# One core, two linear-attention and FFN layer pairs: a new list-scheduling search, a third late q chunk, and the token sum of pk moved from TensorE to Pool

## The chip, the core and the metric

The kernel runs on one core of one Trainium2 chip. The metric is the device time of one execution in microseconds (us); lower is better. In this document PE is TensorE, ACT is ScalarE, DVE is VectorE and Pool is GpSimd.

## The reference

Four residual layers on x of 2048 tokens by 512 features, bf16: attention, FFN, attention, FFN, with the same weights both times (shortened here).

```python
def _A_ref(x, wqkv, wo):                      # H = 32 heads of 16
    q, k, v = ...                             # from x @ wqkv
    phi = lambda t: jnp.where(t > 0, t + 1, jnp.exp(t)) + 1e-6
    pq, pk = phi(q), phi(k)
    kv = jnp.einsum("bhsd,bhse->bhde", pk, v)
    z = jnp.einsum("bhsd->bhd", pk)           # the token sum
    num = jnp.einsum("bhqd,bhde->bhqe", pq, kv)
    den = jnp.einsum("bhqd,bhd->bhq", pq, z)[..., None] + 1e-6
    o = num / den
    return o.transpose(...).reshape(B, S, D) @ wo
# _B_ref: relu(x @ w1) @ w2, Dff = 1376
x = x + _A_ref(_layernorm(x), wqkv, wo)
x = x + _B_ref(_layernorm(x), w1, w2)
# ... and both once more
```

## The kernel before

All operations are collected in a graph with a cost in ns each, and a list scheduler written in Python decides, when the kernel is built, the order on each engine and the PSUM bank of each tile. It starts from the source order and alternates six backward and forward passes.

The tokens are 16 tiles of 128, in four chunks of four. An attention layer has a **key phase** (per tile: the k projection, its phi, and G += xn^T pk; early q chunks in between), a **barrier** (the token sum z, the evacuation of G, kv, Wp = kv @ wo, and the first denominators, none of which can start before the last key tile), and an output phase that overlaps the FFN. q chunks that are projected only in the barrier ("late") are there to give PE something to do. The first layer's key phase also holds the layer norm of the raw input.

phi is two ACT reads of the PSUM bank, then a clamp and a maximum on DVE:

```python
if path == 3:
    g.add(ACT, lambda e: e.activation(dst_ap, psv[:, b, :], ACTF.Identity, bias=1.0 + 1e-6, scale=1.0),
          [("ps", b)], [dst_key], C_ACT_PSUM, name=name + "_lin")
    g.add(ACT, lambda e: e.activation(escr[:, s, :], psv[:, b, :], ACTF.Exp),
          [("ps", b)], [("escr", s)], C_ACT_EXP, name=name + "_exp")
    g.add(DVE, lambda e: e.tensor_scalar(emscr[:, s, :], escr[:, s, :], 1.0, 1e-6, ALU.min, ALU.add),
          [("escr", s)], [("emscr", s)], C_DVE_BF4X, name=name + "_em")
    g.add(DVE, lambda e: e.tensor_tensor(dst_ap, dst_ap, emscr[:, s, :], ALU.max),
          [dst_key, ("emscr", s)], [dst_key], 340.0, name=name + "_phi")
    return
```

The token sum, 64 matmuls of one column per layer, and the barrier:

```python
def a_z_acc(lo, hi, zb):
    def mk():
        mms = []
        for i in range(lo, hi):
            u = pk_unit(i)
            for j in range(4):
                mms.append((psv[:, zb, j:j + 1], big[:, u * 512 + 128 * j:u * 512 + 128 * j + 128], ones[:, 0:1],
                            i == 0 and j == 0, i == NT - 1, True))
        return mms
    mm_group(mk, [("big", pk_unit(i)) for i in range(lo, hi)] + [("ones",)], [("ps", zb)], (hi - lo) * 4 * C_MMTINY, "z%d" % lo)
# [...]
def bar():
    if first_layer:
        den_consts()
    late = list(range(max(0, NCH - Q_LATE), NCH))
    for i in range(NT - LAG, NT):
        a_g_acc(i, GB)
    zb = alloc_bank()
    for k in range(NCH):
        a_z_acc(4 * k, 4 * k + 4, zb)
    a_z_final(zb)
    a_g_evac(GB)
    for t in late[:LATE_A]:
        a_q_proj(t, late=True)
    a_kv()
    for t in range(DEN_PRE):
        a_den(t, GB)
    for t in late[LATE_A:]:
        a_q_proj(t, late=True)
    a_wp()
```

Of the kernel before, what the change touches and what calls it, by code (L numbers as in the profile page):

```python
# [23 lines left out]
C_DVE_PSUM = 600.0  # L24
C_DVE_STT = 615.0
C_DVE_BF4X = 205.0
C_DVE_SMALL = 72.0
C_DVE_BNST = 595.0
C_DVE_NORM_BF = 325.0
C_POOL_POW = 1000.0  # L30
# [6 lines left out]
C_POOL_CP = 700.0  # L37
C_SP_ISSUE = 470.0
TAIL = {PE: 70.0, ACT: 230.0, DVE: 80.0, POOL: 300.0, SP: 0.0}
SYNC_LAT = 40.0  # L40
SLACK = {PE: 0.0, ACT: 0.0, DVE: 0.0, POOL: 0.0, SP: 0.0}


class _Op:
    __slots__ = ("eng", "emit", "reads", "writes", "dur", "lat", "sdeps", "odeps", "idx",
                 "seq", "dma", "name", "t_start", "t_done", "t_ready", "issued", "prio", "alts")

    def __init__(self, eng, emit, reads, writes, dur, lat, dma, name):
        self.eng = eng
        self.emit = emit  # L50
        self.reads = reads
        self.writes = writes
        self.dur = dur
        self.lat = lat
        self.dma = dma
        self.name = name
        self.sdeps = []
        self.odeps = []
        self.alts = None
        self.seq = None  # L60
        self.t_start = None
        self.t_done = None
        self.issued = False
# [100 lines left out]
def _forward(ops, succ, tile_ops, nbanks, fixed_sp):  # L164
# [36 lines left out]
    while remaining:  # L201
        best = None
        fr = sorted(x for x in bank_free if x is not None)
        for e in ENGINES:
            if not ready[e]:
                continue
            fa = free_at[e]
            cands = []
            for o in ready[e]:
                if e == SP and sp_next < len(fixed_sp) and o is not fixed_sp[sp_next]:  # L210
                    continue
                t = o.t_ready
                need = alloc_of.get(o.idx)
                if need:
                    if len(fr) < len(need):
                        continue
                    t = max(t, fr[len(need) - 1] + SYNC_LAT)
                st = max(t, fa)
                if o.alts:
                    mine = [d for (x, _, d) in o.alts if x == e][0]  # L220
                    worse = False
                    for (ae, _, adur) in o.alts:
                        if ae != e and max(t, free_at[ae]) + adur < st + mine - 1e-9:
                            worse = True
                    if worse:
                        continue
                cands.append((st, o))
            if not cands:
                continue
            st0 = min(c[0] for c in cands)  # L230
            lim = st0 + SLACK[e]
            st, o = min((c for c in cands if c[0] <= lim), key=lambda c: (-c[1].prio, c[1].idx))
            if best is None or st0 < best[0] - 1e-9 or (abs(st0 - best[0]) <= 1e-9 and o.idx < best[2].idx):
                best = (st0, st, o, e)
# [28 lines left out]
        if o.dma:  # L263
            dma_free = max(st + 1500.0, dma_free) + o.lat
            o.t_done = dma_free + 500.0
        else:
            o.t_done = st + o.dur + TAIL[e]
# [14 lines left out]

def _list_schedule(ops, tile_ops, vbank, fixed_sp, iters=6, nbanks=8):
    succ = _succs(ops)
    rank = {o.idx: float(o.idx) for o in ops}
    best = None
    for _ in range(iters):
        _backward(ops, succ, rank)
        res = _forward(ops, succ, tile_ops, nbanks, fixed_sp)
        if best is None or res[0] < best[0]:  # L290
            best = res
        for o in ops:
            rank[o.idx] = o.t_start
    total, order, vb, bank_after, snap = best
# [13 lines left out]

def build_kernel(nc, A_x, A_wqkv, A_wo, B_w1, B_w2, out, n_layers_pairs=2, Q_LATE=2, O_PE_CHUNKS=3, PHI_PATH=3,
                 KV_LAG=2, INTERLEAVE=True, WARM=16, SPLIT_CHUNKS=1, TAIL_SPLIT=True,  # L310
                 PHI_K=3, PHI_QE=3, PHI_QL=3, LAST_HALVES=True, ZH_FIRST=True, P2_TIGHT=False,
                 FIRST_PE_CHUNKS=1, TGK=2, TGF=2, WO_LAG=1, DEN_PRE=1, LATE_A=1, ITERS=6):
    S = A_x.shape[1]
# [13 lines left out]
    with es:  # L327
# [46 lines left out]
        rneg = sb("rneg", [128, 1], F32)  # L374
        Zc = sb("Zc", [128, 4, 32], BF16)
        GT = sb("GT", [128, 4, 512], BF16)
        KVT = sb("KVT", [128, 4, 128], BF16)
# [27 lines left out]

        def dma(emit, reads, writes, xfer_ns, name):
            sem = es.enter_context(nc.semaphore("dsem%d" % len(dma_sems)))
            dma_sems.append(sem)

            def _emit(eng, emit=emit, sem=sem):  # L410
                return emit(eng).then_inc(sem, 16)
            op = g.add(SP, _emit, reads, writes, dur=C_SP_ISSUE, lat=xfer_ns, dma=True, name=name)
            op.seq = sem
            return op

        def pk_unit(i):
            return (i % 4) * NCH + (i // 4)
# [21 lines left out]
        ld_x(0, 1)  # L439
        dma(lambda e: e.dma_start(wqkv[:, :, D:2 * D], wq_v[:, :, D:2 * D]), [], [("wk",)], 1600.0, "ld_wk")  # L440
        for t in range(1, NCH):
# [4 lines left out]
        dma(lambda e: e.dma_start(wo[:], A_wo.rearrange("(c p) n -> p c n", p=128)), [], [("wo",)], 1600.0, "ld_wo")  # L446
        early_loads = list(g.ops)
        nfull = NFC - 1 if FLAST < 128 else NFC
# [3 lines left out]
        if FLAST < 128:  # L452
            dma(lambda e: e.dma_start(w2[0:FLAST, NFC - 1, :], B_w2[nfull * 128:DFF, :]), [], [("w2b",)], 600.0, "ld_w2b")
        late_loads = g.ops[len(early_loads):]
        W2KEYS = [("w2a",), ("w2b",)] if FLAST < 128 else [("w2a",)]
# [65 lines left out]
        def tr_dma(lo, hi):  # L521
            dma(lambda e: e.dma_start_transpose(Tb[:, lo:hi, :, :].rearrange("p i c t -> p (i c) t"),
                                                xn[:, lo:hi, :].rearrange("p i d -> p (i d)")),
                [("xn", i) for i in range(lo, hi)], [("T", i) for i in range(lo, hi)], 740.0 * (hi - lo), "tr%d" % lo)

# [96 lines left out]
        def a_k_proj(i):  # L622
            b = alloc_bank()
            mm_group(lambda: [(psv[:, b, :], Tb[:, i, c, :], wqkv[:, c, D:2 * D], c == 0, c == 3, False) for c in range(4)],
                     [("T", i), ("wk",)], [("ps", b)], 4 * C_MM512, "kproj%d" % i)
            phi_evac(b, pk_tile(i), ("big", pk_unit(i)), "k%d" % i, path=PHI_K)

        def a_g_acc(i, GB):
# [4 lines left out]

        def a_z_acc(lo, hi, zb):
            def mk():
                mms = []
                for i in range(lo, hi):
                    u = pk_unit(i)
                    for j in range(4):
                        mms.append((psv[:, zb, j:j + 1], big[:, u * 512 + 128 * j:u * 512 + 128 * j + 128], ones[:, 0:1],  # L640
                                    i == 0 and j == 0, i == NT - 1, True))
                return mms
            mm_group(mk, [("big", pk_unit(i)) for i in range(lo, hi)] + [("ones",)], [("ps", zb)], (hi - lo) * 4 * C_MMTINY, "z%d" % lo)

# [27 lines left out]

        def a_wp():
            for j in range(4):
                b = alloc_bank()
                mm_group(lambda b=b, j=j: [(psv[:, b, :], KVT[:, j, :], wo[:, j, :], True, True, False)],
# [121 lines left out]
        def ln_tile_first(i):  # L798
            ln_stats_first(i)
            c = slice(i, i + 1)  # L800
            g.add(DVE, lambda e: e.tensor_scalar(veps[:, c], mv[:, i, 1:2], 0.0, EPS, ALU.max, ALU.add),
                  [("var", i)], [("veps1", i)], C_DVE_SMALL, name="veps%d" % i)
# [37 lines left out]
        def layer_steps(layer):  # L840
# [3 lines left out]
            if layer % 2 == 0:  # L844
# [13 lines left out]
                def bar():  # L858
# [5 lines left out]
                    zb = alloc_bank()  # L864
                    for k in range(NCH):
                        a_z_acc(4 * k, 4 * k + 4, zb)
                    a_z_final(zb)
# [6 lines left out]
                    for t in late[LATE_A:]:  # L874
                        a_q_proj(t, late=True)
                    a_wp()

                def p2(t):
                    if t < NCH and t >= DEN_PRE:
                        a_den(t, GB)  # L880
                    if t >= WO_LAG:
                        for i in range(4 * (t - WO_LAG), 4 * (t - WO_LAG) + 4):
                            a_wo(i, first_layer)
                        tr_chunk(t - WO_LAG, TGF)
                        ln_ffn(t - WO_LAG)
# [39 lines left out]

        order, total = _list_schedule(g.ops, g.tile_ops, vbank, early_loads + first_tr + late_loads, ITERS)
        for e in (PE, ACT, DVE, POOL):
            for k, o in enumerate(order[e]):
                o.seq = k + 1
# [27 lines left out]

        def emit_engine(e, handle):
            for o in order[e]:
                for d in waits[o.idx]:  # L960
                    if d.dma:
# [10 lines left out]
        with nc.Block() as block:  # L972
# [4 lines left out]
            @block.scalar  # L977
            def _(s):
                s.preload_act_table_set("natural_log_exp_and_others")
                emit_engine(ACT, s)  # L980
# [54 lines left out]
```

## Time and profile before

The median is 295.24 us (295.19 to 295.36), the span in the profile 293.0 us. The lines below are from the profile's page: busy time and share of the span of each engine, and in 40 slices of the span DVE's busy share and the TensorE clock granted, in tenths (9 is 90% or more). PE is busy nearly always, at full clock.

```profile
PE 282.9 (97%) x1470; PEld 129.3 (44%) x1491; DVE 164.0 (56%) x485; ACT 171.8 (59%) x349; POOL 20.7 (7%) x32
...
DVE  5998637996349551480326474599832955130233
...
PEclk9999999999999999999999999999999999999999
```

The next lines are from the PE timeline of before: start us, length us, engine, line, operation and operands, count, and in brackets the idle time before it with what ended it. The token sum occupies PE from 43.98 to the next group at 45.58, 1.60 us. The first barrier follows; at 48.94 and 62.29 PE had been waiting, the second time for 1.43 us.

```profile
43.98 1.74 PE L573 MATMUL ps<-ones,big 128*128 128x1 bf16 x64
45.58 1.05 PE L573 MATMUL ps<-GT,wqkv 128*128 128x128 bf16 x16
...
48.94 0.39 PE L573 MATMUL ps<-wo,KVT 128*128 128x512 bf16 x1 [0.36 <-DVE Wp L652]
...
60.47 0.40 PE L573 MATMUL ps<-big,Zc 128*32 128x512 bf16 x4
62.29 1.89 PE L573 MATMUL ps<-Wp,big 128*128 128x512 bf16 x8 [1.43 <-DVE emscr L557]
```

The view of waits, for PE alone (total us, number of times, longest): it sums both barriers. It counts only time in which no matmul was being executed; by start-to-start distances beyond the regular 0.216 us of a 512-column matmul, PE lost 2.6 us in each barrier.

```profile
PE ps L573 <- DVE emscr L557: 2.9, 2, 1.4
...
PE ps L573 <- DVE Wp L652: 0.7, 2, 0.4
```

The windows view gives the busy us of each engine in stretches of the span (start:end, length, then engine by engine with the number of instructions). 8:44 is the first key phase, 44:66 and 184:206 the barriers.

```profile
core 0: us, PE busy (x) PEld busy (x) DVE busy (x) ACT busy (x) POOL busy (x), PEclk, DMA share, GB/s
8.00:44.00 36.00, 35.57 (x170) 16.03 (x172) 27.71 (x97) 27.82 (x54) 4.71 (x4) 1.00 0.68 187
44.00:66.00 22.00, 20.00 (x170) 9.38 (x171) 20.04 (x53) 19.17 (x42) 0.00 (x0) 1.00 0.25 26
...
184.00:206.00 22.00, 20.00 (x170) 9.43 (x170) 19.70 (x53) 18.84 (x41) 0.00 (x0) 1.00 0.16 25
```

In the groups of instructions (busy us, mean ns of one, then idle time before them), phi's maximum and clamp:

```profile
L559 DVE TENSOR_TENSOR big<-big,emscr 128x512 bf16<-128x512 bf16 x64 | 26.0, 422 | 3.9 <-ACT big L553 3.5
...
L557 DVE TENSOR_SCALAR emscr<-escr 128x512 bf16<-128x512 bf16 x64 | 17.8, 290 | 21.7 <-ACT escr L555 21.2
```

### The profile page before, as it was taken

What the parts mean: (1) busy time and instruction counts of PE and PEld (TensorE: products, weight loads), DVE (VectorE), ACT (ScalarE), POOL (GpSimd) and SP (SyncE); (2) the same over time, 40 slices, a digit from 0 to 9 for tenths busy, and PEclk for the clock granted to TensorE, in tenths of its full rate; (3) what the DMA queues carried; (4) which work ended last, traced back from release to release, by engine and by line L of the source; (5) the groups of instructions that cost most, each with busy time, mean ns of one, the idle gap of its engine ahead of it and who ended that gap; (6) DMA issues with size and microseconds to landing.
All of it is one profiled execution on the core that took longest, in us unless ns stands there. A gap on an engine that the chain in (4) does not pass through costs nothing.

```text
span 293.0 us, 4025 instructions
## 1 busy us (share of the span) xinstructions
PE 282.9 (97%) x1470; PEld 129.3 (44%) x1491; DVE 164.0 (56%) x485; ACT 171.8 (59%) x349; POOL 20.7 (7%) x32
## 2 busy tenths in 40 slices
PE   7999999989999999999999999998999999999996
PEld 2444445434444444444444444533444444444443
DVE  5998637996349551480326474599832955130233
ACT  1888757997664583597623486599766407317000
POOL 4213000002001110010001100000100011000000
PEclk9999999999999999999999999999999999999999
DMA  6945930073003070030000340004610424001022
GB/s 224 346 78 104 303 122 2 0 75 61 10 2 72 0 143 2 1 72 0 3 0 0 72 74 0 2 0 73 39 36 0 34 71 112 0 11 63 0 72 74
DMA packets 40163, 17.23 MB, mean 59 GB/s; under 512 B 31984, under 2 KB 39632, under 8 KB 40144
## 3 DMA queue, kind: packets, MB, share of 16 engines
q1 hardware_dynamic: 40144, 16.98, 26.7%
q8 instruction: 12, 0.20, 0.3%
q14 instruction: 7, 0.06, 0.1%
HBM read 7.01 MB, written 2.10 MB: 31 GB/s over the span
## 4 chain that ended last, share of the span: by engine, by line
PE 83%; DVE 11%; DMA 3%; issue 1%; SPq 0%
PE ps L573 83%; DVE big L720 3%; DMA xin<-in_A_x_dram 2%; DVE xres L586 2%; DMA Tb<-xn 1%; DVE big L559 1%; DVE Wp L652 1%; DVE bst L483 1%; DVE emscr L557 1%; DVE xn L593 1%; DVE rsp L714 1%; DVE rhi L713 0%; DVE xn L515 0%; DVE nmf L589 0%; DVE xin L760 0%
## 5 line engine op out<-in xcount | busy, mean ns | idle before, releaser
L573 PE MATMUL ps<-Tb,w 128*128 128x512 bf16 (+1 forms) x352 | 78.0, 379 | 0.0
L573 PE MATMUL ps<-w,big 128*128 128x512 bf16 (+3 forms) x355 | 76.4, 372 | 0.4
L741 ACT ACTIVATE big<-ps 128x512 bf16<-128x512 f32 (+1 forms) x81 | 48.2, 596 | 29.4 <-PE ps L573 28.9
L580 ACT ACTIVATE sqscr<-xres 128x512 bf16<-128x512 f32 x48 | 30.3, 635 | 42.7 <-DVE xres L617 27.9
L573 PEld LDWEIGHTS ps<-w,big 128*128 128x128 bf16 (+1 forms) x363 | 35.4, 98 | 40.8
L573 PEld LDWEIGHTS ps<-Tb,w 128*128 128x128 bf16 (+1 forms) x352 | 34.9, 100 | 40.9 <-issue 0.9
L555 ACT ACTIVATE escr<-ps 128x512 bf16<-128x512 f32 x64 | 38.4, 613 | 9.7 <-PE ps L573 9.7
L553 ACT ACTIVATE big<-ps 128x512 bf16<-128x512 f32 x64 | 38.3, 613 | 3.0 <-PE ps L573 3.0
L613 DVE SCALAR_TENSOR_TENSOR xin<-ps,rstdf,xres 128x512 bf16<-128x512 f32 x15 | 11.3, 750 | 38.5 <-PE ps L573 38.5
L573 PE MATMUL ps<-wqkv,Tb 128*128 128x512 bf16 x125 | 31.4, 379 | 0.3
L573 PE MATMUL ps<-Wp,big 128*128 128x512 bf16 x124 | 28.7, 379 | 3.0 <-DVE emscr L557 2.9
L573 PE MATMUL ps<-big,xn 128*128 128x512 bf16 x124 | 31.3, 379 | 0.2
L573 PE MATMUL ps<-Tb,wqkv 128*128 128x512 bf16 x128 | 30.5, 380 | 0.1
L557 DVE TENSOR_SCALAR emscr<-escr 128x512 bf16<-128x512 bf16 x64 | 17.8, 290 | 21.7 <-ACT escr L555 21.2
L559 DVE TENSOR_TENSOR big<-big,emscr 128x512 bf16<-128x512 bf16 x64 | 26.0, 422 | 3.9 <-ACT big L553 3.5
L617 DVE SCALAR_TENSOR_TENSOR xres<-ps,rstdf,xres 128x512 f32<-128x512 f32 x16 | 12.0, 751 | 24.8 <-PE ps L573 24.8
L720 DVE TENSOR_TENSOR big<-big,ps 128x512 bf16<-128x512 bf16 x32 | 20.1, 681 | 7.9 <-PE ps L573 7.9
L573 PEld LDWEIGHTS ps<-Wp,big 128*128 128x128 bf16 x128 | 12.2, 98 | 17.6 <-DVE big L720 3.0
L573 PEld LDWEIGHTS ps<-big,xn 128*128 128x128 bf16 x128 | 12.5, 98 | 15.1 <-DVE big L559 0.2
L573 PEld LDWEIGHTS ps<-wqkv,Tb 128*128 128x128 bf16 x128 | 12.2, 98 | 15.2 <-DMA Tb<-xn 0.6
L573 PEld LDWEIGHTS ps<-Tb,wqkv 128*128 128x128 bf16 x128 | 11.7, 98 | 15.3 <-issue 1.8
L606 POOL TENSOR_TENSOR rstdf<-varf,nhalf 128x4 f32<-128x4 f32 x8 | 8.1, 1007 | 144.6 <-DVE varf L604 144.6
(76 smaller groups left out, 180.7 us busy)
## 6 DMA issues: line engine op xcount, KB each, us to landing
wqkv<-in_A_wqkv_dram SPq DMA_DIRECT2D x3, 512.0 KB, 6.9
xin<-in_A_x_dram SPq DMA_DIRECT2D x3, 512.0 KB, 7.9
out_dram<-xin SPq DMA_DIRECT2D x3, 512.0 KB, 2.9
w<-in_B_w_dram SPq DMA_DIRECT2D x1, 1376.0 KB, 6.3
w<-in_B_w_dram SPq DMA_DIRECT2D x1, 1280.0 KB, 9.8
wo<-in_A_wo_dram SPq DMA_DIRECT2D x1, 512.0 KB, 8.6
Tb<-xn SPq DMA_TRANSPOSE x30, 3.2
xin<-in_A_x_dram SPq DMA_DIRECT2D x1, 384.0 KB, 3.3
```

The source lines that it names most:

```text
L553: g.add(ACT, lambda e: e.activation(dst_ap, psv[:, b, :], ACTF.Identity, bias=1.0 + 1e-6, scale=1.0), [("ps", b)], [dst_key], C_ACT_PSUM, ...
L555: g.add(ACT, lambda e: e.activation(escr[:, s, :], psv[:, b, :], ACTF.Exp), [("ps", b)], [("escr", s)], C_ACT_EXP, name=name + "_exp")
L557: g.add(DVE, lambda e: e.tensor_scalar(emscr[:, s, :], escr[:, s, :], 1.0, 1e-6, ALU.min, ALU.add), [("escr", s)], [("emscr", s)], C_DVE_B ...
L559: g.add(DVE, lambda e: e.tensor_tensor(dst_ap, dst_ap, emscr[:, s, :], ALU.max), [dst_key, ("emscr", s)], [dst_key], 340.0, name=name + "_ ...
L573: last = e.matmul(o, l, r, start=st, stop=sp, skip_group_check=skip)
L580: g.add(ACT, lambda e: e.activation(sqscr[:, q, :], xres[:, i, :], ACTF.Square, accum_out=dst[:, i:i + 1]), [("xres", i)], [("sqscr", q), ...
L586: g.add(DVE, lambda e: e.scalar_tensor_tensor(xres[:, i, :], psv[:, b, :], 0.0, src, ALU.add, ALU.add, accum_out=s1f[:, i:i + 1]), [("ps", ...
L606: g.add(POOL, lambda e: e.tensor_tensor(rstdf[:, sl], varf[:, sl], nhalf[:, 0:4], ALU.pow), [("varf", t), ("nhalf",)], [("rstdf", t)], C_P ...
L613: g.add(DVE, lambda e: e.scalar_tensor_tensor(xin[:, i, :], psv[:, b, :], rstdf[:, i:i + 1], xres[:, i, :], ALU.mult, ALU.add), rd, [("xin ...
L617: g.add(DVE, lambda e: e.scalar_tensor_tensor(xres[:, i, :], psv[:, b, :], rstdf[:, i:i + 1], xres[:, i, :], ALU.mult, ALU.add, accum_out= ...
L720: g.add(DVE, lambda e, j=j: e.tensor_tensor(unit_ap(us[j]), unit_ap(us[j]), psv[:, GB[j], :], ALU.mult), [("big", us[j]), ("ps", GB[j])], ...
L741: g.add_flex([(ACT, lambda e, M=M, b=b, u=u: e.activation(unit_ap(u, M), psv[0:M, b, :], ACTF.Relu), C_ACT_PSUM), (DVE, lambda e, M=M, b=b ...
```

## The change

Its intent: take 48 of the 64 one-column matmuls off PE in each attention layer, by summing the first twelve pk tiles in f32 on Pool (11 adds) and giving the sum to PE as a bf16 high and low part (8 matmuls); move a third of the four q chunks into the barrier, to fill the waits there; put Wp into the four PSUM banks of G; and search longer for an order, with random ranks and a little slack. The start uses 12 warm-up matmuls instead of 16. The local search (SEARCH) is added but switched off. The core of the diff:

```diff
-SLACK = {PE: 0.0, ACT: 0.0, DVE: 0.0, POOL: 0.0, SP: 0.0}
+SLACK = {PE: 60.0, ACT: 100.0, DVE: 150.0, POOL: 0.0, SP: 0.0}
[... cost constants, the search with random ranks ...]
-def build_kernel(..., Q_LATE=2, ..., WARM=16, ..., ITERS=6):
+def build_kernel(..., Q_LATE=3, ..., WARM=12, ..., WP_GB=True, ..., ITERS=12, SEARCH=0, ZP=3, ...):
[...]
+            if 0 < i < 4 * ZP:
+                prev = pk_tile(0) if i == 1 else zacc[:, :]
+                pkey = ("big", pk_unit(0)) if i == 1 else ("zacc",)
+                g.add(POOL, lambda e: e.tensor_tensor(zacc[:, :], prev, pk_tile(i), ALU.add),
+                      [("big", pk_unit(i)), pkey], [("zacc",)], C_POOL_TT, name="zp%d" % i)
+                if i == 4 * ZP - 1:
+                    g.add(POOL, lambda e: e.tensor_copy(zhl[:, 0, :], zacc[:, :]), ...)
+                    g.add(POOL, lambda e: e.tensor_tensor(zhl[:, 1, :], zacc[:, :], zhl[:, 0, :], ALU.subtract), ...)
[...]
-                    for k in range(NCH):
-                        a_z_acc(4 * k, 4 * k + 4, zb)
+                    if ZP:
+                        a_z_acc(-2, 0, zb, True)
+                    for k in range(ZP, NCH):
+                        a_z_acc(4 * k, 4 * k + 4, zb, k == 0)
[...]
-                b = alloc_bank()
+                b = GB[j] if WP_GB else alloc_bank()
```

## The prediction

> **What bounds it now.** TensorE. The page shows PE busy 97% of 293.0 us at full granted clock; the chain that ended last is 83% PE. In the PE timeline, 128x512 matmuls start every 0.216 us, almost without gaps, from 12.6 us to 290 us. Only removed PE work or closed PE gaps can pay.
>
> **Where PE has gaps.** By start-to-start times: about 2 us before 10 us (layer norm of the first tiles), 0.26 us at 18.5 us (first DMA transposes), and in each of the two attention barriers (44 to 65 us and 184 to 205 us): 0.52 + 0.24 us at Wp, 0.17 us before the reciprocal broadcast, and 1.5 us before the first late output projection. That is 2.4 us per barrier, 4.9 us in all. The windows view shows why: in 44 to 65 us PE is busy 19.0, DVE 19.0 and ACT 18.2 of 21 us. All three are nearly full.
>
> **Removed.** The token sum: 64 one-column matmuls take 1.60 us (43.98 to 45.58), 0.025 us each. The new order keeps 24 per layer (8 from the hi/lo pair, 16 from the last chunk): 0.6 us. Saved 1.0 us a layer, 2.0 us in all, straight on the PE chain. The shorter warm-up saves nothing: PE waits for VectorE afterwards.
>
> **Added.** Per attention layer 11 Pool adds, one copy and one subtract of 128x512. The Trainium skill, "GPSIMD Engine Reference", section Performance versus the Vector engine, gives 4497 ns for a 2048-wide f32 add; a quarter plus start-up is my estimate of 1.2 to 1.3 us, about 16 us of Pool per layer. In layer 1 the adds should start near 18.5 us, the low half be ready near 36.5 us; PE wants it near 39 us. The same page says Pool shares an SBUF interface with VectorE, which exposes the phi maximum (0.42 us) and clamp (0.29 us). No trace here shows how much. If the adds took 1.5 us, PE would wait about 1 us.
>
> **Moved.** A third q chunk (16 matmuls, 3.46 us) goes from the key phase into the barrier as filler. It also brings four phi evacuations: ACT 8 x 0.61 = 4.9 us, VectorE 4 x 0.71 = 2.8 us. ACT then needs about 23 us against 21.5 us of PE work, with four free PSUM banks. By hand, with trace durations, I still find about 2 us of PE waits per barrier (Wp 0.5, a bank 0.3, second reciprocal broadcast 1 us), so I credit 0.4 us per barrier. At the start ACT normalises tile 0, so the first key projection comes about 0.6 us sooner, but the transposes landing near 18.2 us instead of 18.9 us take most of that back: net 0 to 0.3 us.
>
> **Sum.** -2.0 (token sum) - 0.8 (barriers) - 0.2 (start) - 0.2 (other) = -3.2: 292.0 us. Range 289.7 to 294.6. Faster by over 2%: 0.08; within 2%: 0.90; slower: 0.02.
>
> **What would show it.** One-column matmuls 128 to 48, their two groups 0.6 us each; Pool busy 20.7 to about 50 us; Pool adds near 1.25 us; no PE wait on the hi/lo tile; barrier waits still 1.5 to 2.5 us each, ended by ACT or VectorE.
>
> **What would make it wrong.** Faster: the search closes nearly all barrier waits (up to 4 us more). Slower: Pool and VectorE block each other, so phi tiles and transposes come late in the first key phase, or the low half comes after PE wants it; or ACT holds PSUM banks in the barrier and opens larger PE gaps.

## More of the kernel before

In the barriers PE, DVE and ACT are all nearly full; in the first key phase DVE has 8 us free.

## The result

The changed kernel took 293.84 us (293.50 to 294.24, four runs) against 295.22 us of the kernel before in the same rounds; ratio 0.9953, 95% interval 0.9936 to 0.9971. All ratios here are the mean time of one kernel's runs over that of the other's in the same rounds, so not quite the ratio of the quoted medians. The gain is 1.4 us; 3.2 us had been predicted.

The profile after, in the same views. The page (this run kept no clock records, so it has no clock row, and the 1.00 in the clock column of its windows, below, is only a default; its matmuls start 0.216 us apart, as before); DVE is now full in slices 2 to 6:

```profile
PE 280.4 (96%) x1386; PEld 126.4 (43%) x1407; DVE 184.7 (63%) x479; ACT 176.1 (60%) x355; POOL 50.0 (17%) x58
...
DVE  5999996999628591386336587799863955130233
```

The PE timeline. The token sum is now two short groups. Apart from 0.26 us between these two groups, PE runs through the whole barrier without a wait over 0.13 us; before it, in the key phase, PE waits for phi:

```profile
23.15 1.04 PE L617 MATMUL ps<-big,xn 128*128 128x512 bf16 x4 [0.56 <-DVE big L603]
...
25.78 1.04 PE L617 MATMUL ps<-big,xn 128*128 128x512 bf16 x4 [0.73 <-DVE big L603]
...
30.50 1.04 PE L617 MATMUL ps<-big,xn 128*128 128x512 bf16 x4 [0.66 <-DVE big L603]
...
43.28 0.34 PE L617 MATMUL ps<-ones,zhl 128*128 128x1 bf16 x8
43.73 0.55 PE L617 MATMUL ps<-ones,big 128*128 128x1 bf16 x16
...
53.68 1.03 PE L617 MATMUL ps<-Tb,wqkv 128*128 128x512 bf16 x4
54.63 3.63 PE L617 MATMUL ps<-Wp,big 128*128 128x512 bf16 x16
```

The waits of PE: those of the barriers are gone, and six waits for phi's maximum (L603, which was L559) are new.

```profile
PE ps L617 <- DVE big L603: 3.4, 6, 0.7
...
PE ps L583 <- DVE xn L559: 1.1, 1, 1.1
PE ps L583 <- ACT xn L557: 1.0, 1, 1.0
PE ps L617 <- ACT Tb L587: 0.7, 1, 0.7
```

The windows. DVE is busy 34.5 of 36 us in the first key phase, 6.8 us more than before, although it runs fewer instructions there (86 against 97); PE is busy 4.4 us less there, somewhat more than it gained in the two barriers (1.9 us each).

```profile
8.00:44.00 36.00, 31.20 (x162) 13.73 (x164) 34.52 (x86) 24.72 (x47) 18.34 (x17) 1.00 0.66 187
44.00:66.00 22.00, 21.95 (x131) 9.77 (x130) 18.96 (x50) 19.73 (x39) 0.00 (x0) 1.00 0.13 25
...
184.00:206.00 22.00, 21.89 (x119) 9.85 (x120) 21.11 (x57) 21.54 (x45) 0.00 (x0) 1.00 0.13 25
```

The groups of phi's maximum and clamp, and of the new adds. Same count, same shapes, but the maximum takes 550 ns on average instead of 422, the clamp 362 instead of 290. The Pool adds take 1.21 us, as had been estimated.

```profile
L603 DVE TENSOR_TENSOR big<-big,emscr 128x512 bf16<-128x512 bf16 x64 | 34.0, 550 | 2.8 <-ACT big L597 1.2
L601 DVE TENSOR_SCALAR emscr<-escr 128x512 bf16<-128x512 bf16 x64 | 22.5, 362 | 10.7 <-ACT escr L599 10.2
```

```profile
L674 POOL TENSOR_TENSOR zacc<-zacc,big 128x512 f32<-128x512 f32 x20 | 24.2, 1211 | 25.7 <-DVE big L603 24.0 <-DVE esel L750 1.5
```

Why a mean of 550 ns: the individual instructions fall into two classes. Here is one stretch of the timeline, Pool and DVE together (the lines of the other engines are left out). A Pool add starts at 30.58; the normalisation that DVE starts at 30.69, 0.40 us a few lines earlier at 29.38, takes 1.25 us and ends just after the add. The same with the add at 32.94 and the maximum at 33.03 (1.34 us). In the whole trace 11 maxima started inside a full-width Pool instruction, and every one of them ended 0.28 us after it.

```profile
29.38 0.40 DVE L559 TENSOR_SCALAR xn<-xin,rstd,nbias 128x512 bf16<-128x512 bf16 x1
...
30.58 1.21 POOL L674 TENSOR_TENSOR zacc<-zacc,big 128x512 f32<-128x512 f32 x1 [1.35 <-DVE big L603]
30.69 1.25 DVE L559 TENSOR_SCALAR xn<-xin,rstd,nbias 128x512 bf16<-128x512 bf16 x1
...
32.38 0.41 DVE L603 TENSOR_TENSOR big<-big,emscr 128x512 bf16<-128x512 bf16 x1
...
32.94 1.15 POOL L674 TENSOR_TENSOR zacc<-zacc,big 128x512 f32<-128x512 f32 x1 [1.15 <-DVE big L603]
...
33.03 1.34 DVE L603 TENSOR_TENSOR big<-big,emscr 128x512 bf16<-128x512 bf16 x1
```

Where the time went, by milestones of the PE timeline (start of the group, us). The changed kernel has 24 fewer 512-column matmuls ahead of the first token sum (16 of q, 8 of G), which is 24 x 0.216 = 5.2 us of work moved behind it.

| milestone | before | after | what it says |
|---|---|---|---|
| first key matmul | 8.26 | 7.50 | -0.8 us: the first tile's layer norm is ordered better |
| first token sum | 43.98 | 43.28 | the key phase took 35.8 us for work that took 35.7 - 5.2 = 30.5 before: +5.3 us |
| first FFN output matmul | 89.28 | 90.92 | from the token sum: 47.6 against 45.3 + 5.2 - 1.0 (fewer one-column matmuls): -1.9 us |
| second token sum | 184.32 | 180.96 | |
| FFN output after the second barrier | 229.62 | 228.38 | from the previous FFN milestone 137.5 against 140.3: -2.9 us, of which 1.0 is the token sum and 1.9 the barrier |
| last matmuls | 290.04 | 288.81 | -1.2 us in all |

So the change gains 2.0 us from the token sum, 3.7 us from the two barriers and 0.8 us at the start, and gives 5.3 us back in the first key phase. (The waits that vanish from each barrier are 2.6 us, its net gain is 1.9 us: 0.2 to 0.3 us came back as the wait inside the token sum, and some 0.4 us in short pauses that were not followed up.)

### The profile page after: what moved, and what is told of

The parts are those of the page before. It is cut to its first block, busy times and chain, and to the rows that moved or that the text cites. A ratio compares the mean times of both kernels' runs of the same rounds, so it can differ in the third digit from the quotient of the medians.

```text
span 291.8 us, 3890 instructions
## 1 busy us (share of the span) xinstructions
PE 280.4 (96%) x1386; PEld 126.4 (43%) x1407; DVE 184.7 (63%) x479; ACT 176.1 (60%) x355; POOL 50.0 (17%) x58
## 4 chain that ended last, share of the span: by engine, by line
PE 80%; DVE 10%; ACT 5%; DMA 2%; issue 1%; SPq 0%; DVEq 0%
PE ps L617 80%; DVE big L603 4%; ACT big L597 2%; DMA xin<-in_A_x_dram 2%; ACT escr L599 2%; DVE emscr L601 2%; DVE bst L527 2%; DVE xn L559 2%; DVE nbias L549 1%; ACT big L796 1%; ACT lden L766 0%; DVE mv L528 0%; ACT Tb L587 0%; DVE xin L815 0%; SPq L484 0%
## 5 line engine op out<-in xcount | busy, mean ns | idle before, releaser
L617 PE MATMUL ps<-w,big 128*128 128x512 bf16 (+2 forms) x356 | 76.4, 372 | 0.4
L796 ACT ACTIVATE big<-ps 128x512 bf16<-128x512 f32 (+1 forms) x78 | 46.2, 599 | 27.4 <-PE ps L617 27.0
L603 DVE TENSOR_TENSOR big<-big,emscr 128x512 bf16<-128x512 bf16 x64 | 34.0, 550 | 2.8 <-ACT big L597 1.2
L601 DVE TENSOR_SCALAR emscr<-escr 128x512 bf16<-128x512 bf16 x64 | 22.5, 362 | 10.7 <-ACT escr L599 10.2
L674 POOL TENSOR_TENSOR zacc<-zacc,big 128x512 f32<-128x512 f32 x20 | 24.2, 1211 | 25.7 <-DVE big L603 24.0
L661 DVE SCALAR_TENSOR_TENSOR xres<-ps,rstdf,xres 128x512 f32<-128x512 f32 x16 | 12.0, 750 | 22.3 <-PE ps L617 22.1
L617 PEld LDWEIGHTS ps<-big,xn 128*128 128x128 bf16 x128 | 11.7, 97 | 19.6 <-DVE big L603 6.8
```

The lines of the kernel that those rows point to most:

```text
L617: last = e.matmul(o, l, r, start=st, stop=sp, skip_group_check=skip)
L661: g.add(DVE, lambda e: e.scalar_tensor_tensor(xres[:, i, :], psv[:, b, :], rstdf[:, i:i + 1], xres[:, i, :], ALU.mult, ALU.add, accum_out= ...
L674: g.add(POOL, lambda e: e.tensor_tensor(zacc[:, :], prev, pk_tile(i), ALU.add), [("big", pk_unit(i)), pkey], [("zacc",)], C_POOL_TT, name= ...
L796: g.add_flex([(ACT, lambda e, M=M, b=b, u=u: e.activation(unit_ap(u, M), psv[0:M, b, :], ACTF.Relu), C_ACT_PSUM), (DVE, lambda e, M=M, b=b ...
```

## The experiments

**Theory 1.** While a Pool instruction streams its operands, a DVE instruction that needs the second SBUF interface stands still until the Pool instruction ends. phi and the normalisations of the first layer come late, and PE waits for them. **Theory 2.** The first key phase lost its filler: without the second q chunk, PE asks for phi faster than DVE can make it, whatever Pool does. Two smaller questions: what closed the barriers (the third late chunk, the shared banks, the search), and whether Pool's mere time (layer-norm roots queued behind adds) rather than its streaming does the harm.

In the table, "key waits" is the sum of the start-to-start distances beyond 0.216 us in the first key phase after the start-up (12 us on), each over 0.13 us, and "barrier waits" the same for each barrier, from the profiled run. (A distance of exactly twice 0.216 us is a matmul record missing from the trace, and is not counted.) phi is the mean of the maximum on DVE. The kernel before took 295.2 us in the rounds of the changed kernel, 295.55 in those of e1 to e4, 295.21 in those of e5 to e8 and 295.10 in those of e9 to e11; across these groups compare the ratios.

| kernel | median us | ratio to before (95%) | key waits us | barrier waits us | phi ns |
|---|---|---|---|---|---|
| before | 295.2 | 1 | 0.3 | 2.6 / 2.6 | 422 |
| changed | 293.84 | 0.9953 (0.9936-0.9971) | 4.4 | 0 / 0 | 550 |
| e1 small adds (wrong result) | 289.01 | 0.9782 (0.9767-0.9797) | 0.2 | 0 / 0 | 422 |
| e2 no Pool sum | 291.20 | 0.9851 (0.9833-0.9868) | 0 | 0 / 0 | 422 |
| e3 two late chunks | 297.01 | 1.0053 (1.0034-1.0071) | 3.4 | 1.9 / 1.9 | 564 |
| e4 Pool sum in the second layer only | 290.24 | 0.9819 (0.9803-0.9835) | 0 | 0 / 0 | 484 |
| e5 two late chunks, no Pool sum | 296.09 | 1.0034 (1.0003-1.0066) | 0.3 | 2.2 / 1.8 | 423 |
| e6 adds in four pieces | 292.46 | 0.9905 (0.9889-0.9920) | 2.0, and 1.3 for the hi/lo pair | 0 / 0 | 475 |
| e7 e4 with own banks for Wp | 292.25 | 0.9892 (0.9874-0.9911) | 0 | 1.2 / 0.7 | 506 |
| e8 e4 with the old search | 291.45 | 0.9868 (0.9851-0.9885) | 0 | 1.2 / 0.3, and 0.5 in the second token sum | 504 |
| e9 adds replaced by powers (wrong result) | 289.13 | 0.9801 (0.9781-0.9822) | 0.2 | 0 / 0 | 430 |
| e10 e2 with adds that nobody reads | 294.96 | 1.0001 (0.9974-1.0027) | 4.0 | 0 / 0 | 564 |
| e11 e4 with the local search | 291.88 | 0.9890 (0.9870-0.9909) | 0.8 | 0 / 0 | 474 |

### e1: the same order, small adds

The order on every engine is that of the changed kernel, instruction for instruction; only the adds are narrow.

```diff
-                g.add(POOL, lambda e: e.tensor_tensor(zacc[:, :], prev, pk_tile(i), ALU.add),
+                w = 512 if i == 1 else 8
+                g.add(POOL, lambda e: e.tensor_tensor(zacc[:, 0:w], prev[:, 0:w], pk_tile(i)[:, 0:w], ALU.add),
```

> The changed kernel with the same order on every engine, but ten of the eleven Pool adds of a layer 8 columns wide instead of 512 (wrong result on purpose; the first add, the copy and the subtract stay whole). Theory 1 (while a Pool instruction runs, a VectorE instruction with two SBUF inputs or in a fast copy mode stands still, so phi and normalisation come late): VectorE's phi maximum falls from a mean of 550 ns to 420-460, the PE waits between 20 and 38 us fall from about 4.4 us to under 1 us, time about 289.5 us (288.5 to 290.5). Theory 2 (the first key phase is short of PE filler because the second q chunk was moved out, and VectorE's own work sets the pace): waits stay above 3 us, time about 293.

Measured 289.01 us, phi 422 ns, 0.2 us of key waits. PE's waits from the profile, all of them before the first 12 us:

```profile
PE ps L583 <- DVE xn L559: 1.4, 1, 1.4
PE ps L508 <- DVE wrm L501: 1.2, 1, 1.2
PE ps L617 <- ACT Tb L587: 0.7, 1, 0.7
```

With the order held fixed, the width of ten adds per layer is worth 4.3 us of span (291.8 to 287.5). Theory 2 predicted about 293 us and is refuted.

### e2: no Pool sum

```diff
-ITERS=12, SEARCH=0, ZP=3,
+ITERS=12, SEARCH=0, ZP=0,
```

> The changed kernel with the whole token sum back on TensorE (no Pool adds), three late q chunks kept; the order is searched anew. Theory 1: key-phase waits of PE under 1 us, barriers as gapless as in the changed kernel, 1.0 us more PE work per layer: about 291.3 us (290.3 to 292.5). Theory 2: key-phase waits stay near 4 us and the matmuls come on top: about 295.5.

Measured 291.20 us, no key waits, no barrier waits: three late chunks, without the Pool sum, leave the key phase gapless. The 2.2 us over e1 are about the 2 x 1.0 us of one-column matmuls. This run also says what the Pool sum is worth in the changed kernel: with it the kernel takes 293.84 us, without it 291.20, so it costs about 2.6 us more than it saves (3.0 us by the ratios).

### e3: two late chunks, Pool sum kept

```diff
-n_layers_pairs=2, Q_LATE=3,
+n_layers_pairs=2, Q_LATE=2,
```

> The changed kernel with two late q chunks as before the change, Pool sum kept. Theory 1: the adds still hold VectorE up, phi mean stays above 520 ns, and PE waits in the first key phase of 1 to 4 us remain (less than now, as 3.5 us of filler is back); barrier waits of 1 to 2.5 us come back in each layer: 293 to 296 us. Theory 2: key-phase waits under 1 us, barrier waits back: 290 to 292.5 us.

Measured 297.01 us, a little beyond the range of theory 1 and far from theory 2. Filler back in the key phase did not help: 2.9 of the 3.4 us of key waits are one wait, for ACT to free a PSUM bank: ACT had waited 1.1 us for DVE's clamp to free its scratch buffer, and in front of that clamp DVE had a maximum of 1.28 us and two normalisations that took 1.66 us together, under two Pool adds. Both barriers wait 1.9 us again. Why it lies past the range stays open. One thing that I had not expected is the clock of the profiled execution: PE stood idle for 1.8 us after its twelve warm-up matmuls, and the windows view shows the granted clock (after Pool's column) at 0.59 from 8 to 12 us. But that is not the whole of it: the two executions with a mean clock of 1.0 took 296.42 and 296.47 us, past the range too; of the four with 0.994, this one took 296.44 us and the others 297.6.

```profile
6.00:8.00 2.00, 0.56 (x6) 0.40 (x7) 1.74 (x9) 0.25 (x1) 1.63 (x3) 0.96 1.04 345
8.00:12.00 4.00, 4.00 (x21) 1.94 (x20) 3.65 (x13) 3.33 (x6) 0.21 (x1) 0.59 1.08 361
12.00:16.00 4.00, 4.00 (x22) 1.74 (x20) 3.71 (x9) 3.84 (x8) 1.98 (x2) 1.00 0.76 233
```

### e4: the Pool sum in the second attention layer only

```diff
+                zp = 0 if first_layer else ZP
-                    if ZP:
+                    if zp:
                         a_z_acc(-2, 0, zb, True)
-                    for k in range(ZP, NCH):
+                    for k in range(zp, NCH):
```

(and the adds of a tile are made only where `zp` is not 0)

> The changed kernel with the Pool sum in the second attention layer only; the first keeps its 64 matmuls. Theory 1: the first key phase loses its waits (over 3.5 us of 4.4) and pays 1.0 us for the matmuls: about 290.3 us (289.3 to 291.3), faster than both kernels. Theory 2: about 294.5 us.

Measured 290.24 us, correct, ratio 0.9819: faster than both kernels, and within the expected range. In the second layer DVE is held up just as much (phi 484 ns over both layers, so about 2 x 484 - 422 = 546 in that one), but there DVE has no layer norm of raw tiles to make at the pace of PE (in the changed kernel it is busy 22.3 us of the 36 from 148 to 184 us, against 34.5 in the first key phase), and PE never waits for it. PE's waits in e4; after 12 us there is none in this list:

```profile
PE ps L508 <- DVE wrm L501: 1.2, 1, 1.2
PE ps L617 <- ACT Tb L587: 0.7, 1, 0.7
PE ps L583 <- DVE xn L559: 0.5, 1, 0.5
PE ps L583 <- ACT xn L557: 0.3, 1, 0.3
```

### e5: two late chunks, no Pool sum

```diff
-n_layers_pairs=2, Q_LATE=3,
+n_layers_pairs=2, Q_LATE=2,
-ITERS=12, SEARCH=0, ZP=3,
+ITERS=12, SEARCH=0, ZP=0,
```

> The changed kernel with neither the Pool sum nor the third late q chunk; what is left of the change is the new search. If the third chunk is what closed the barriers: PE waits of 1.5 to 2.5 us per barrier are back, the key phase has none, about 294.8 us (294 to 296). If the new search closed them: no barrier waits, about 291.2 us as with three late chunks and no Pool sum.

Measured 296.09 us (294.76 to 298.10), just past the range. The barrier waits are back, 2.2 and 1.8 us; what is left of the change without the third chunk (the search, the shared banks, the shorter warm-up) is no gain by the median. The times spread more than elsewhere, and the slower executions have a mean granted clock of 0.988 to 0.994: the same loss of clock after the warm-up as in e3. The quickest, 294.76, has 0.999; it is 0.45 us below the median of before in the same rounds.

### e6: each add in four pieces of 128 columns

```diff
+                def _add4(e):
+                    last = None
+                    for q in range(0, 512, 128):
+                        last = e.tensor_tensor(zacc[:, q:q + 128], prev[:, q:q + 128], pk_tile(i)[:, q:q + 128], ALU.add)
+                    return last
-                g.add(POOL, lambda e: e.tensor_tensor(zacc[:, :], prev, pk_tile(i), ALU.add),
+                g.add(POOL, _add4,
```

> The changed kernel with the same order, each Pool add cut into four of 128 columns. If VectorE can take the SBUF interface between two Pool instructions: its longest phi maximum falls from 1.34 us to about 0.8, its mean below 500 ns, PE waits between 20 and 38 us below 4 us, 291.5 to 293.3 us, unless four starts make Pool so slow that the low half comes late. If Pool keeps it through back-to-back instructions: phi mean at or above 550 ns, 294 to 297 us.

Measured 292.46 us: DVE does get in between. Of the maxima that started inside a piece, 25 in number, the median is 530 ns and the longest 655, and of 23 such clamps the median is 511 ns. But four pieces take Pool 4 x 0.50 = 2.0 us instead of 1.21 us for one add, the low half comes late, and PE waits 1.1 us for it:

```profile
PE ps L617 <- DVE big L603: 1.3, 4, 0.6
...
PE ps L617 <- POOL zhl L683: 1.1, 1, 1.1
```

### e7 and e8: what else closed the barriers

Both start from e4. e7 undoes the sharing of G's banks; e8 puts the old search back (no slack, six rounds, no random ranks; the new cost constants stay).

```diff
# e7
-FT_PE=0, WP_GB=True,
+FT_PE=0, WP_GB=False,
# e8
-SLACK = {PE: 60.0, ACT: 100.0, DVE: 150.0, POOL: 0.0, SP: 0.0}
+SLACK = {PE: 0.0, ACT: 0.0, DVE: 0.0, POOL: 0.0, SP: 0.0}
-LATE_A=1, ITERS=12,
+LATE_A=1, ITERS=6,
-sigma = rng.choice((0.0, 0.0, 200.0, 600.0, 2000.0)) if k >= 4 else 0.0
+sigma = 0.0
```

> The version with the Pool sum in the second attention layer only, with Wp evacuated from freshly allocated PSUM banks as before the change instead of the four of G. If sharing G's banks helped to close the barriers: PE waits of 0.5 to 2 us per barrier, 291.2 to 294 us. If the third late chunk alone did it: no waits, 289.8 to 290.8 us.

> The version with the Pool sum in the second attention layer only, with the old search (six rounds, no random ranks, no slack). If the random search and the slack matter: PE waits of 0.5 to 2 us more in all, 290.8 to 292.5 us. If they don't: within 0.4 us of 290.2.

e7: 292.25 us, with waits of 1.2 and 0.7 us in the barriers. e8: 291.45 us, with 1.2 and 0.3 us there, and 0.5 us in front of the second token sum's last part. So the third late chunk does the larger part (e5 and e3: 1.8 to 2.2 us per barrier without it), and the shared banks (1.2 and 0.7 us) and the search (1.2 and 0.3) less. Each of these builds is a new order on all engines, so the split between them is rough: e7 also starts 0.4 us later.

### e9: Pool equally busy, but not streaming

Again the order of the changed kernel. Its output is wrong, which doesn't matter for the time. Ten adds per layer become an 8-column add and a power of 128x4 elements.

```diff
+                    e.tensor_tensor(zacc[:, 0:8], prev[:, 0:8], pk_tile(i)[:, 0:8], ALU.add)
+                    return e.tensor_tensor(pdum[:, :], onesf[:, 0:4], nhalf[:, 0:4], ALU.pow)
```

> The changed kernel with the same order, ten of the eleven Pool adds of a layer replaced by an 8-column add and a power of 128x4 elements, so that Pool is busy about as long (near 1.1 us) but streams almost nothing (wrong result on purpose). If what stops VectorE is the stream of Pool's operands through the shared SBUF interface: phi maximum near 420-460 ns on average, key-phase waits under 1 us, about 289.3 us as with the small adds alone. If it is Pool's time itself (the reciprocal square roots of the layer norm queue behind the adds, or any running Pool instruction holds VectorE): waits and time as in the changed kernel, 292.5 to 294 us.

Measured 289.13 us, key waits 0.2 us. Pool was busy as long as with the adds (0.26 + 1.06 us for each), and DVE did not notice:

```profile
L679 POOL TENSOR_TENSOR pdum<-onesf,nhalf 128x4 f32<-128x4 f32 x20 | 21.2, 1058 | 0.0
...
L678 POOL TENSOR_TENSOR zacc<-zacc,big 128x8 f32<-128x8 f32 x20 | 5.2, 258 | 18.0 <-DVE big L604 17.2 <-DVE esel L756 0.2
```

```profile
L604 DVE TENSOR_TENSOR big<-big,emscr 128x512 bf16<-128x512 bf16 x64 | 26.3, 430 | 3.2 <-ACT big L598 1.9
```

So it is not Pool's time, nor the layer norm's roots queueing behind it, but the streaming of 512-column operands.

### e10: the adds alone

e2, plus the eleven adds, the copy and the subtract on Pool, read by nobody. The result is right.

```diff
-            if 0 < i < 4 * ZP:
+            if 0 < i < 12:
-                if i == 4 * ZP - 1:
+                if i == 11:
```

> The kernel without the Pool sum, with three late chunks (291.2 us), plus the eleven adds, copy and subtract on Pool again, whose result nobody reads (right result). If the adds themselves cost the time: key-phase waits of 3 to 5 us are back and the time rises by 3 to 5 us to 294.3-296.3. If the loss came from TensorE waiting for the hi/lo pair or from the order that its dependence gave: under 1 us more, 291 to 292.2.

Measured 294.96 us (294.29 to 296.63), 3.8 us over e2 (4.4 by the ratios), with 4.0 us of key waits. No engine waits for the result, and still the loss is there in full. (The profiled run also lost clock at the start, 0.994 in the mean; the executions with 1.0 took 294.3 to 295.8 us.)

### e11: the local search switched on

```diff
-ITERS=12, SEARCH=0,
+ITERS=12, SEARCH=150,
```

on top of e4.

> The version with the Pool sum in the second attention layer only, with 150 steps of the new local search that the change added but leaves off. Only start-up waits of about 2 us are left to close, so 289.2 to 290.8 us, no more than 1 us from 290.2; if the model that guides the search is off on the chip, it may as well be slower, up to 291.5.

Measured 291.88 us, slower than e4 and just outside both guesses. The order that the search's own model likes better has 0.8 us of key waits in the first layer, and 1.4 us of new waits in the second key phase (165 to 178 us), where the Pool adds are (the maxima there took 1.2 to 1.3 us); a model that does not know that Pool holds DVE up can't see them. That this is why was not tested.

## Why the prediction was wrong

The number was wrong by two terms of opposite sign that were both mis-sized, and half cancelled; that the total came as near as it did is luck.

- **Token sum, -2.0 us: right.** 64 one-column matmuls became 24, 1.60 us became 0.6 us; in the first layer the 16 of the last chunk waited 0.26 us for the last phi.
- **Pool adds of 1.2 to 1.3 us: right.** 1.21 us in the mean. The estimate came from the Trainium skill, "GPSIMD Engine Reference", section Performance versus the Vector engine (4497 ns at 2048 columns), and this trace agrees with it. The low half was ready at 41.9 us instead of 36.5, because pk itself came late; PE reached it at 43.3 and did not wait.
- **The sum had no term for Pool holding DVE up: the failed step.** The prediction named the shared interface as a risk ("which exposes the phi maximum (0.42 us) and clamp (0.29 us)") and entered 0 us. The runs put about 4 us there (e1: 4.3 us with the order fixed; e10: 3.8 us). The Trainium skill has this, and I had not looked it up where it stands: "SBUF — State Buffer", section Who interferes with whom, says that a DVE instruction with two SBUF inputs contends with a Pool instruction that reads SBUF, and that whoever issues first keeps the shared pair for the whole instruction. This trace agrees, with numbers: 11 maxima that started inside a full-width Pool instruction took 0.77 to 1.34 us, against 0.42 us alone, while the 5 maxima and 9 clamps that were running when a Pool instruction started kept their length (0.41 to 0.42 and 0.28 to 0.29 us). (One normalisation that started 0.02 us before an add was held all the same, for 1.33 us.) Six of the eight clamps that started inside one (0.29 us alone, then 0.69 to 1.25), the normalisation (0.40 to 1.25 us) and layer norm's 4-element instruction with two SBUF inputs (0.13 to 1.11 us) are hit the same way. The input statistics (one SBUF input: 681 against 685 ns) and an addition from PSUM (751 ns both ways, one case) are not.
- **Barriers, -0.8 us: wrong, -3.7 us.** The hand count kept about 2 us of waits per barrier; after the token sum none over 0.13 us was left. In "ACT then needs about 23 us against 21.5 us of PE work" one size is wrong: it charged ACT 0.61 us per PSUM read, the length of one record in the profile. Back-to-back reads start every 0.477 us (some 0.494), in the trace of before as in that of after, so twelve late q tiles cost ACT 24 x 0.477 = 11.4 us, not 14.6. In the second barrier of the changed kernel ACT is busy 21.5 of 22 us and PE 21.9: ACT is full, but it keeps up. That this charge is why the count kept its 2 us is argued, not shown. e3 and e5 show that the third chunk is needed to close the barriers, e7 and e8 that the shared banks and the search are needed too.
- **Start, -0.2 us: partly.** The first key matmul came 0.8 us earlier, as said (0.6), but PE then waited 1.1 us for the fourth tile's normalisation. Even without the wide adds (e1) the key phase ran 1.3 us longer than the work moved out of it explains; most of it is in that wait.

## What to carry to other kernels

Before moving work to Pool, list the DVE instructions that will run meanwhile and are of the kinds held up here (two SBUF inputs; clamp and normalisation, which read one SBUF tile), and charge each the rest of the Pool instruction; if DVE sets the pace there (here: the first key phase, DVE 27.7 of 36 us busy before), leave it on PE. The same move did no harm in a phase where DVE had room: keeping the Pool sum in the second layer alone gave 290.24 us, the best right result. When adding up a busy engine, use start-to-start distances, not the lengths of the records, or the engine looks fuller than it is.

## What the Trainium skill lacked or had wrong

- "SBUF — State Buffer", section Who interferes with whom: it says that the first to issue keeps the shared pair for the whole instruction. A Pool power of 128x4 elements, which also reads SBUF and runs 1.0 us, did not hold DVE: in the profile of e9, 18 maxima that started inside one took 410 to 454 ns and 15 clamps 279 to 294 ns, as when alone; the page does not have this exception.
- The same page gives no size of the loss for small operands: a 4-element DVE instruction with two SBUF inputs took 1.11 us instead of 0.13 us behind a Pool add, and sat on the layer norm's chain. Nor does it say that cutting the Pool instruction lets DVE in between (e6: maximum 530 ns in the median, at 0.50 us per quarter add).
- "ScalarE: Activation LUTs", section What ACT_TABLE_LOAD costs: it says that back-to-back ACTIVATEs overlap by about 93 ns. Reads of a PSUM bank of 512 columns took 613 ns each and mostly started every 477 ns: an overlap of 136 ns.
- "TensorE: Matmul & The Clock Gate", section What's actually happening: it gives the cold clock after one idle window of about 3.4 us. In e3, PE was idle for 1.8 us after 4.3 us of warm-up, and the clock fell to half for 3.4 us all the same (0.59 in the mean from 8 to 12 us), though in the 3.4 us before the fall PE was busy about half of the time; in the kernel before, with 0.7 us idle at that place, it did not. The length of the idle time alone does not decide it: in e6, 1.8 us of idle from 8.9 to 10.7 us cost no clock.
